# Another issue order for a fused attention and two-MLP kernel on one Trainium2 core

## The chip, the cores and the metric

The kernel runs on one core of one Trainium2 chip. The metric is the device time of one execution in microseconds (us), as a median over runs; the profile is one further execution, taken by the hardware profiler. The engines are TensorE (PE in the rows, with its weight loads as PEld), VectorE (DVE), ScalarE (ACT), GpSimd (POOL) and SyncE (SP, which issues every DMA here).

## What is computed

8192 tokens of width 192 go through three stages:

```python
# 1. attention: per head a softmax over 7 taps, then a causal sum of 7 shifted rows
w = exp(weight_gen - max); w = w / (sum(w) + 1e-9)
x = einsum('bshk,bskhg->bshg', w, x_unf).reshape(8192, 192)
# 2. first MLP
h = x @ moe_w_in            # 192 -> 2048
x = (h / (1 + exp(-h))) @ moe_w_out
# 3. second MLP, its activation a ratio of polynomials
h = x @ moe2_w_in
P = a0 + a1*h + a2*h**2 + a3*h**3
Q = 1 + |b0|*|h| + |b1|*h**2
out = (P / (Q + 1e-6)) @ moe2_w_out
```

The weights arrive as 64-bit floats and are decoded on the chip.

## The kernel before

The tokens are cut into 16 blocks of 512. For every block `attention` (L691) builds the weighted sums, `unit1` (L911) runs the first MLP in 8 units of 256 hidden channels, `between` (L932) hands its result over, `unit2` (L953) runs the second MLP in 8 units, and `finish` (L1016) stores. Every fp32 factor is split in a high and a low part; a product is the sum of three matmuls per weight.

Each step of this is registered once as a named operation with `Plan.op`. The names that the text uses, with u a unit and b a block, written u.b:

- attention: `M`, `m` (products of taps and rows, L742, on POOL or DVE), `p`, `r`, `a` (their sums, L752, L756, L762, on DVE or POOL), `T` and `TR` (the two halves of a transpose on PE, L822), `XH`/`XL` (high and low part of the transposed block, `XH0`/`XL0` for the first MLP on tile tp, `XH1`/`XL1` for the second on tile acc; ACT L839, DVE L843);
- first MLP: `A`, `K` (the two halves of the first product into bank h, PE), `S` (silu, ACT L916), `H`, `L` (high and low part, ACT L920, DVE L924), `C`, `E`, `I`, `F` (second product into acc, PE);
- second MLP: `B`, `Q` (first product), `U`, `V` (ACT L961, L965), `u`, `w`, `Y` (DVE L971, L974, L980), `N`, `G` (ACT L985, L988), `g` (DVE L991), `h`, `l` (high part on POOL, ACT or DVE, low part on DVE or POOL, L1001), `D`, `P`, `J`, `R` (second product);
- decoding of weights, `q` + MLP + matrix + part: `l0`/`l1` loads by DMA, `a0`/`a1` the top bits (ACT L603), `40`/`41` the joining into a PSUM bank (tile dec, DVE L616), `h` the high part (ACT; for matrix B in two steps `h0` and `h1`, L656 and L657), `x` the low part (DVE L637; `x0` and `x1` for matrix B). `q1B` is the 64-row remainder of the second MLP's first matrix;
- softmax chunks `s0` to `s5`, constants `cl`, `ca`, `cr`, `cn`, `cz`.

The order in which all 3956 operations are issued is the string `ORDER` (L40), one entry per operation: `^` or `^^` puts a load of ScalarE's function table before it, `@n` picks the n-th of the engines that the operation allows, `:x` names the buffer slot of a tile that appears there first, and `<n` or `>n` shifts a matmul group of the one half of PE's rows against the other. Each engine runs its own operations in this order, and waits where an input or a buffer is not ready. There are eight PSUM banks in four slots of two (A to D); the tiles h, acc, dec, tp and to share them, so a new tile in a slot waits for the last reader of the tile before.

PE works as two halves of 64 rows, each with its own 64x128 weights, side by side. `Lanes` (L376) merges two queues, one per half, by counted turns. The two row halves must not add into one bank half at the same time, so where a group turns a bank from one side to the other, an empty instruction on SP (L405, `sp.nop`) waits for both halves of the first side, and the second side waits for it:

```python
            if was:
                while any(self.left[n] for n in was[2]):
                    self.take(1 - r)
                step = self.sp.nop()
```

## Time and profile before

| | |
|---|---|
| median of 3 runs | 1211.11 us (1210.18 to 1213.15) |
| the profiled execution | 1208.21 us, of which the span from first to last instruction is 1206.4 us |
| PE matmul busy | 1171.9 us (97%) in 10332 instructions |
| PE weight loads busy | 1038.9 us (86%) |
| DVE busy | 1082.1 us (90%) in 1023 instructions |
| ACT busy | 1035.7 us (86%) in 1011 instructions |
| POOL busy | 508.0 us (42%) in 335 instructions |
| mean granted TensorE clock | 0.996 of full speed |

A matmul's end is modelled, and two of them, one per row half, run at the same time; a busy PE therefore tells that at least one half works.

### The profile page before, as it was taken

What the parts mean: (1) busy time and instruction counts of PE and PEld (TensorE: products, weight loads), DVE (VectorE), ACT (ScalarE), POOL (GpSimd) and SP (SyncE); (2) the same over time, 40 slices, a digit from 0 to 9 for tenths busy, and PEclk for the clock granted to TensorE, in tenths of its full rate; (3) what the DMA queues carried; (4) which work ended last, traced back from release to release, by engine and by line L of the source; (5) the groups of instructions that cost most, each with busy time, mean ns of one, the idle gap of its engine ahead of it and who ended that gap; (6) DMA issues with size and microseconds to landing.
All of it is one profiled execution on the core that took longest, in us unless ns stands there. A gap on an engine that the chain in (4) does not pass through costs nothing.

```text
span 1206.4 us, 24906 instructions
## 1 busy us (share of the span) xinstructions
PE 1171.9 (97%) x10332; PEld 1038.9 (86%) x10332; DVE 1082.1 (90%) x1023; ACT 1035.7 (86%) x1011; POOL 508.0 (42%) x335
## 2 busy tenths in 40 slices
...
GB/s 218 215 129 58 50 1 14 43 1 64 1 38 49 42 23 34 23 17 23 1 56 24 34 60 1 11 55 1 23 1 43 31 1 42 2 24 1 10 1 40
DMA packets 17753, 45.42 MB, mean 38 GB/s; under 512 B 2412, under 2 KB 9194, under 8 KB 17640
## 3 DMA queue, kind: packets, MB, share of 16 engines
...
## 4 chain that ended last, share of the span: by engine, by line
PE 78%; DVE 5%; ACT 4%; issue 1%; POOL 1%; SPq 0%; DMA 0%; DVEq 0%; ACTq 0%; POOLq 0%
PE acc L809 40%; PE h L809 37%; DVE y L980 1%; POOL g2l L1001 1%; DVE t L971 1%; DVE t L974 1%; PE to L1029 1%; ACT y L988 1%; PE tp L822 1%; DVE t L991 1%; ACT y L985 1%; ACT g2h L465 0%; ACT y L965 0%; ACT t L961 0%; ACT g1h L920 0%
## 5 line engine op out<-in xcount | busy, mean ns | idle before, releaser
L809 PE MATMUL h<-xh,wa 64*128 64x512 f32 x2048 | 437.9, 393 | 7.7 <-DVE t L974 4.1
L809 PEld LDWEIGHTS h<-xh,wa 64*128 64x128 f32 x2048 | 277.7, 184 | 44.6 <-SPq L405 7.4
L809 PE MATMUL h<-xh,wb 64*128 64x512 f32 x1024 | 296.9, 388 | 0.0
L809 PE MATMUL h<-xl,wa 64*128 64x512 f32 x1024 | 296.6, 388 | 0.1
L809 PE MATMUL acc<-g2h,wo 64*128 64x512 f32 x1536 | 287.5, 390 | 1.3 <-ACT g2h L465 1.0
L809 PE MATMUL acc<-g1h,wo 64*128 64x512 f32 x1536 | 287.6, 392 | 0.2
L1001 POOL TENSOR_TENSOR g2l<-t,g2h 128x1024 fp32r<-128x1024 f32 x76 | 195.0, 2570 | 136.1 <-ACT g2h L465 36.6
L809 PEld LDWEIGHTS acc<-g2h,wo 64*128 64x128 f32 x1536 | 208.3, 184 | 19.6 <-SPq L405 1.7
L809 PEld LDWEIGHTS acc<-g1h,wo 64*128 64x128 f32 x1536 | 205.2, 185 | 19.1 <-ACT g1h L920 1.2
L809 PE MATMUL acc<-g2l,wo 64*128 64x512 f32 x1024 | 201.4, 391 | 0.1
L809 PE MATMUL acc<-g1l,wo 64*128 64x512 f32 x1024 | 197.0, 394 | 0.2
L924 DVE TENSOR_TENSOR g1l<-h,g1h 128x1024 fp32r<-128x1024 f32 x128 | 155.8, 1220 | 41.3 <-ACT g1h L920 35.9
L980 DVE SCALAR_TENSOR_TENSOR y<-y,b_sb 128x1024 f32<-128x1024 f32 x128 | 175.9, 1381 | 5.6 <-ACT y L965 5.0
L467 POOL TENSOR_SCALAR g2h<-t 128x1024 fp32r<-128x1024 f32 x56 | 68.3, 1223 | 266.2 <-DVE t L991 108.4
L971 DVE TENSOR_TENSOR t<-t,h 128x1024 f32<-128x1024 f32 x128 | 155.3, 1215 | 26.1 <-ACT t L961 13.2
L991 DVE SCALAR_TENSOR_TENSOR t<-t,a_sb,y 128x1024 f32<-128x1024 f32 x128 | 168.4, 1328 | 8.3 <-ACT y L988 7.7
L742 POOL TENSOR_TENSOR pr<-xw,aw 128x576 f32<-128x576 f32 (+1 forms) x73 | 114.4, 1580 | 140.1 <-PE acc L809 83.3
L961 ACT ACTIVATE t<-h,a_sb 128x1024 f32<-128x1024 f32 x128 | 153.8, 1203 | 18.2 <-PE h L809 14.9
L916 ACT ACTIVATE h<-h 128x1024 f32<-128x1024 f32 x128 | 129.3, 1012 | 44.3 <-PE h L809 40.7
L974 DVE SCALAR_TENSOR_TENSOR t<-t,a_sb,h 128x1024 f32<-128x1024 f32 x128 | 163.5, 1279 | 3.7
L965 ACT ACTIVATE y<-h,b_sb 128x1024 f32<-128x1024 f32 x128 | 141.8, 1111 | 25.9 <-PE h L809 20.0
L809 PEld LDWEIGHTS h<-xh,wb 64*128 64x128 f32 x1024 | 149.6, 184 | 10.1
...
## 6 DMA issues: line engine op xcount, KB each, us to landing
...
```

What stands on the lines that cost most here:

```text
L467: pool.tensor_scalar(out=out, in0=in_, scalar1=1.0, scalar2=0.0, op0=ALU.mult, op1=ALU.add)
L742: e.tensor_tensor(out=p.rearrange("p k (h g) -> p k h g", g=G), in0=st[xw][:, j + k0:j + k0 + n, :].rearrange("p k (h g) -> p k h g", g=G) ...
L809: return pe.matmul(out=out, lhsT=w, rhs=x, start=start, stop=stop)
L916: act.activation(out=st[hb], in_=st[hb], func=AF.Silu)
L924: dve.tensor_tensor(out=t, in0=st[hb], in1=st[gh].bitcast(F32), op=ALU.subtract)
L961: act.activation(out=q, in_=st[hb], func=AF.Identity, scale=a_sb[:, 3:4], bias=a_sb[:, 2:3])
L965: act.activation(out=q, in_=st[hb], func=AF.Abs, scale=b_sb[:, 1:2])
L971: dve.tensor_tensor(out=st[t], in0=st[t], in1=flat(), op=ALU.mult)
L974: dve.scalar_tensor_tensor(out=st[t], in0=st[t], scalar=a_sb[:, 1:2], in1=flat(), op0=ALU.add, op1=ALU.mult)
L980: dve.scalar_tensor_tensor(out=st[y], in0=st[y], scalar=b_sb[:, 0:1], in1=st[y], op0=ALU.add, op1=ALU.mult)
L991: dve.scalar_tensor_tensor(out=st[t], in0=st[t], scalar=a_sb[:, 0:1], in1=st[y], op0=ALU.add, op1=ALU.mult)
L1001: e.tensor_tensor(out=q, in0=st[t], in1=st[gh].bitcast(F32), op=ALU.subtract)
```

## The change

Only the string `ORDER` changes; the operations and all functions are the same. Counted in the two strings:

- The operations of every engine come in another order, from the second entry on. 3956 entries stay 3956.
- Loads of ScalarE's function table: 79 before, 89 after.
- Choice of engine: `h` on POOL/ACT/DVE 56/43/29 before, 54/49/25 after; `l` on DVE/POOL 52/76, then 55/73; `p` on DVE/POOL 34/30, then 28/36; `r` on DVE/POOL 30/34, then 25/39; `a` on POOL/DVE 45/19, then 42/22; `M` on POOL/DVE 36/28, then 37/27; `m` 37/27, then 39/25; the evacuations `EC` and `FC` on ACT/DVE 26/6, then 22/10.
- In PE's program, a bank turned to its other side directly after the last matmul of the first side: 16 times before, 7 after. Turns in all: 684 and 669. Neighbouring matmuls or transposes that use the same row half: 224 and 192; from PE's 9600th instruction on, where the program drains, 32 and 12.
- In the decoding of `q1B`, ACT's `h0` stood before DVE's `x1` and now stands behind it. Between `XL0.0` and `q1B0x0` DVE loses M0.1, M1.1, m2.1, r0.1, r1.1 and s1m and receives p0.1, p1.1, p2.1, a3.1, q0O140 and q1O040.
- Up to `XL1.1`, the entry of block 1 into the second MLP, DVE loses M0.1, M1.1, m2.1, m0.3, m2.3, p0.3, p1.3, p2.3, r0.1, r1.1, r1.2, r1.3, s1m, Y7.0, g4.0, g6.0, h2.0 and l0.0 and receives a3.1, a0.2, a2.2, l5.0, p0.1, p1.1, p2.1, p2.2, r3.2 and q0O140. The matmuls ahead of some groups: `T.1` 282 before and 280 after, `B0.0` 376 and 376, `B1.1` 877 and 854, of 9728 in all.
- At the start, `q0B0l1` is loaded ahead of the own rows of block 0 (`Z.0`), and `s2l` behind them. Ahead of `XL0.0` DVE loses s0n and r3.0 (to POOL) and q0O140 (to a later place) and receives s1m.

The start, up to about block 0's entry into the second MLP, and the end, before and after:

```diff
--- before.py
+++ after.py
@@ -38,247 +38,246 @@
-    s0l X.0 s2l:r q0B0l0:x s0m s0d ^^s0e Z.0 cn cz:f s0t s0n M1.0@1:i M0.0@1:y s2m M2.0@1:a q0B0l1:e q0A0l0:h q0B0a0
-    q0B040:B q0A0a0 q0A0l1:l m1.0@1:o q0O0l0:n M3.0@1:q m0.0@1:d p0.0 p1.0 r0.0 m3.0@1:u q0A040:C q0B0a1 q0B041 r1.0
-    a0.0@1:s m2.0@1:m p3.0 r3.0 p2.0 q0A0a1 q0A041 q0O0a0 r2.0 q0O040:D q0B0h0 a2.0 W0.0:A q0B0h1 a3.0 a1.0 q0B0x0
-    q0B0x1 q0A0h q0A0x q0O1l0:j WT.0 q0O0l1:e q0O1a0 q0O0a1 s2d@1 q0O140:C q0O041 XH0.0:d XL0.0:b s1l q0O1l1:m
-    q0A1l1:v W1.0:B s1m q0O1a1 A0.0 q0O141 q0O0h q0A1l0:t q0O0x s1d@1 A1.0:A cl X.1 K0.0 s2e q0O1h@1 s1e s1t q0O1x
-    ^S0.0 s2t s1n@1 K1.0 H0.0:h L0.0:m S1.0 H1.0:n L1.0:w A2.0:D I0.0:C q0O2l1:i K2.0>2 s2n@1 q0O2l0:k q0A1a1 q0A1a0
-    m1.1:p C0.0>2 A3.0:B C1.0 E1.0<2 ca S2.0 H2.0:a E0.0<2 q0A140:A K3.0<2 q0O3l0:q m0.1:h F1.0<2 q0A141 I1.0<2 I2.0
-    L2.0:o F2.0>2 q1O0l0:l q0A1h q0A1x s2s A5.0:A>2 q0O3l1:w q0O2a0 q1B0l1:u q0O2a1 S3.0 E2.0>1 K5.0>1 m3.1:c
-    q0O240:D F0.0 H3.0:j M0.1@1:e I3.0 q0O241 L3.0:y p0.1@1 M2.1:v q0O2h q0O2x S5.0 H5.0:k cr m2.1@1:g A4.0:B>2
-    L5.0:n p2.1@1 q1A0l1:t q1B0l0:s q0O3a0 C2.0>2 q1A0l0:m q0O340:D q0O3a1 q0O341 K4.0 S4.0 M3.1@1:a q0O3h q0O3x
-    A6.0:A C3.0 K6.0<2 E3.0<2 p3.1@1 M1.1@1:w A7.0:D<1 H4.0:h S6.0 H6.0:j C4.0<1 L4.0:i q1O1l0:g K7.0<3 L6.0:q
-    q1B0a0 X.2 q1B0a1 AW.2 C6.0<3 E6.0<3 p1.1@1 E5.0<3 r3.1@1 S7.0 H7.0:c q1B040:B q1B041 r1.1 r0.1 r2.1 q1B0h1 I6.0
-    F4.0>2 F5.0>2 q1A0a1 L7.0:u q1A0a0 a0.1:x F7.0 I4.0 F6.0>2 a3.1 a1.1 F3.0>2 I5.0>2 a2.1 q1O0l1:r q1O1l1:p q1B0h0
-    q1B0x1 E4.0 q1A1l0:b q1A1l1:e q1A040:A q1A041 q1B0x0 q1A0h T.1:B TR.1 I7.0 m0.2:d E7.0 m2.2:t C7.0 C5.0<2 q1O0a0
-    q1O0a1 q1A0x q1O040:D q1O041 q1O1a0 q1O1a1 q1O0h q1O140:A q1O141 q1O0x m3.2:g XH0.1:q XL0.1:y A2.1:D K2.1 q1A1a0
-    q1O1h EC.0:c q1O1x m1.2:a q1A1a1 M3.2:p EM.0 A1.1:A q1A140:B q1A141 S2.1 H2.1:u s3l:o q1A1h AW.3 q1O2l0:n K1.1
-    p3.2 L2.1:j A0.1:D K0.1 r3.2@1 S1.1 EA.0 XH1.0:h q1O2l1:x q1A1x H1.1:c XL1.0:i M0.2:w A3.1:B K3.1 M2.2:k p0.2@1
-    M1.2:v L1.1:s B0.0:C Q0.0 s3m S0.1 q1O2a0 H0.1:g S3.1 H3.1:l q1O2a1 q1O3l0:d q1O240:A L0.1:e r0.2@1 L3.1:b
-    p1.2@1 B5.0:D F1.1:B F2.1 V0.0:a a0.2:n Q5.0 q1O241 r1.2 q1O3l1:x Y0.0 E2.1 E0.1 E3.1 q1O2h X.3 q1O2x U0.0:r
-    B3.0:A F0.1 U5.0:w Q3.0 u0.0 u5.0 I2.1 F3.1>2 w0.0 a1.2 ^^N0.0 w5.0 B2.0:C>2 q1O3a1 U3.0:j p2.2@1 r2.2@1 a3.2
-    u3.0 C2.1>2 G0.0 a2.2 s3d@1 E1.1 q1O3a0 g0.0 V3.0:e V5.0:b Q2.0 m3.3:t w3.0 I1.1 q1O340:D m2.3@1:u I3.1>2
-    h0.0@1:p B1.0:A>2 U2.0:k q1O341 q1O3h Y5.0 q1O3x C1.1>2 Q1.0 V2.0:a u2.0 U1.0:m u1.0 N5.0 w2.0 s3e s3t m1.3:f
...
-    V4.15:j Y4.15 h5.15@1:l u4.15 w4.15 Q7.15>4 h6.15@1:h N4.15 FC.14:n G4.15 l5.15@1:e V7.15:w U7.15:y D5.15>3
-    D3.15 P3.15<2 l6.15:b P5.15 g4.15 Y7.15 u7.15 h4.15@1:f l4.15@1:s N7.15 G7.15 w7.15 g7.15 h7.15@2:w l7.15:p
-    D6.15 P6.15<1 R6.15 J5.15 FT.14:C>2 R5.15>2 J4.15>2 J6.15>4 R4.15 O.13 D4.15 P4.15<2 D7.15<1 P7.15 FR.14 R7.15
-    J7.15 FE.14@1 FA.14 O.14 FC.15:v FT.15:D FR.15 FE0.15 FA0.15 FE1.15@1 O0.15 FA1.15 O1.15
+    s0l cz:f s0m X.0 q0B0l0:h q0B0l1:x Z.0 s0d ^^s0e s0t s0n@1 M2.0@1:a M1.0@1:l q0B0a0 q0B040:B M0.0@1:q q0B0a1
+    q0B041 q0B0h0 m2.0@1:h m0.0@1:r M3.0@1:u m3.0@1:w q0B0h1 m1.0@1:e p2.0 p0.0 r2.0 p1.0 q0A0l0:b q0A0a0 cn
+    q0A040:C W0.0:A r0.0 r1.0 cl q0A0l1:s q0A0a1 q0A041 p3.0 a0.0@1:g s1l q0O0l0:n q0O0a0 ca r3.0@1 a1.0 q0B0x0 a3.0
+    a2.0 q0A0h q0A0x q0O040:D q0B0x1 s2l:k q0O0l1:d q0O1l0:t q0O0a1 q0O1l1:v WT.0 W1.0:B s1m q0O041 q0A1l0:h q0O1a0
+    q0A1l1:e s2m s1d@1 XH0.0:r XL0.0:y cr s2d@1 q0O140:C q0O1a1 q0O0h q0O0x q0O141 s1e s1t q0O1h@1 s2e X.1 q0O1x
+    A0.0 A1.0:A q0A1a0 K0.0 ^S0.0 H0.0:l L0.0:t q0O2l0:c A2.0:D K1.0 S1.0 H1.0:q s1n@1 L1.0:w K2.0 I0.0:C q0O2l1:x
+    q0A140:A S2.0 q0A1a1 q0A141 H2.0:v m3.1:h m1.1:j A3.0:B q0A1h L2.0:d q0A1x q0O3l0:n q0O2a0 I1.0 F0.0>2 F1.0>2
+    K3.0>2 E1.0>2 q1B0l1:a q1B0l0:i S3.0 q0O240:D M3.1@1:o C0.0>2 C1.0 A5.0:A<1 q0O2a1 q0O241 p3.1@1 H3.0:u q0O2h
+    L3.0:l q0O2x F2.0 q0O3a0 q0O3l1:p m0.1:b K5.0 I3.0 F3.0>2 A4.0:B>2 q0O340:D q1A0l0:x C3.0>2 s2t S5.0 H5.0:w K4.0
+    q1B0a0 q1O0l0:s q1A0l1:c q0O3a1 L5.0:m M2.1:g E2.0 E0.0 A6.0:A m2.1:n C5.0 K6.0<2 p2.1 q0O341 F5.0<2 I2.0<2 I5.0
+    S4.0 H4.0:e r2.1 L4.0:t F4.0>2 M1.1:p q1B040:B q0O3h q1B0a1 q0O3x S6.0 A7.0:D>2 q1O0l1:i C2.0>2 q1O1l1:u
+    q1O1l0:d r3.1@1 q1A0a0 H6.0:h q1B041 p1.1 q1B0h1 q1A0a1 K7.0 E4.0 S7.0 H7.0:v E5.0 E3.0 C4.0 M0.1:a L6.0:q
+    C6.0<2 q1A040:A C7.0<4 p0.1 q1A041 q1B0x1 q1A1l0:c r0.1@1 a0.1:j q1A1l1:m L7.0:r q1O0a0 r1.1@1 a3.1@1 q1O040:D
+    q1B0h0 a1.1 q1B0x0 q1O0a1 a2.1 q1A0h F6.0 q1O041 q1A0x q1O0h q1O0x q1O1a0 I6.0 T.1:B q1O140:A s3l:o E7.0 E6.0
+    TR.1 XH0.1:q q1O1a1 F7.0 XL0.1:s q1O141 I7.0 I4.0>2 q1A1a0 EC.0:g q1O1h q1A140:B q1O1x A2.1:D q1A1a1 q1A141
+    q1O2l1:w K2.1 S2.1 s3m H2.1:c EM.0 L2.1:n q1O2l0:t A1.1:A K1.1 q1A1h q1O3l1:d q1O2a1 S1.1 EA.0 XH1.0:h H1.1:p
+    X.2 A0.1:D K0.1 S0.1 H0.1:a q1A1x XL1.0:i s3d@1 q1O2a0 L1.1:x s2n@1 L0.1:g s2s A3.1:B K3.1 S3.1 H3.1:l B0.0:C
+    q1O240:A q1O241 B5.0:D q1O2h q1O3a1 L3.1:y Q0.0 V0.0:e q1O2x Q5.0 E1.1:B C3.1 V5.0:b C1.1<2 U5.0:w AW.2 B3.0:A<4
+    U0.0:v Y0.0 Y5.0 m1.2:t M1.2:u I2.1<4 F1.1<1 q1O3l0:r Q3.0<1 M0.2:m ^^N0.0 U3.0:j F0.1<1 q1O3a0 V3.0:k m2.2:x
+    u5.0 u0.0 w0.0 w5.0 I0.1<1 I1.1>1 B2.0:C>3 q1O340:D u3.0 m0.2:p q1O341 p0.2@1 F2.1>3 F3.1>3 w3.0 Q2.0>3 C0.1>3
...
+    V7.15:p l2.15:h U7.15:n g3.15 B4.15:C h3.15@1:g J2.15 R2.15>2 J5.15>2 Y7.15 N7.15 G7.15 Q4.15>4 V4.15:d R6.14>4
+    P2.15>4 D3.15>4 D2.15>2 l3.15@1:l P5.15 P3.15 U4.15:y u7.15 w7.15 g7.15 R3.15 h7.15@1:s Y4.15 l7.15@1:a N4.15
+    G4.15 u4.15 w4.15 g4.15 h4.15@2:r l4.15:k R6.15 J3.15 R5.15>2 J7.15>2 R7.15 FC.14:t FT.14:C P7.15 D7.15 D4.15<2
+    P4.15 FR.14 R4.15 J4.15 FC.15:u FT.15:D FE.14@1 FA.14 O.14 FR.15 FE1.15 FA1.15 O1.15 FE0.15 FA0.15 O0.15
```

## Rows read from the trace of the kernel before

**Rows 1.** By stretch: us, busy (count) PE, PEld, DVE, ACT, POOL, PEclk, DMA, GB/s
```profile
29.00:85.00 56.00, 50.94 (x392) 39.73 (x394) 49.34 (x70) 45.60 (x58) 32.12 (x29) 0.97 0.60 180
85.00:148.00 63.00, 61.73 (x521) 50.42 (x519) 60.83 (x61) 58.83 (x60) 37.64 (x25) 1.00 0.18 59
148.00:1140.00 992.00, 984.15 (x8815) 885.79 (x8811) 892.66 (x810) 868.66 (x830) 408.70 (x260) 1.00 0.08 24
1140.00:1206.40 66.40, 59.39 (x504) 47.82 (x502) 56.17 (x50) 50.04 (x49) 22.76 (x10) 0.97 0.07 23
```

**Rows 2.** Waits: engine, line, what it awaited; us in total, times, longest
```profile
DVE wb L637 <- ACT wb L657: 2.9, 1, 2.9
PE tp L822 <- DVE t L974: 2.9, 1, 2.9
```

**Rows 3.** PE in time around 68 us: start us, us, engine line op names; idle before
```profile
67.97 1.02 PE L822 MATMUL tp<-ident,ao 64*128 64x64 f32 x16 [2.94 <-DVE wb L637]
...
73.48 0.49 PE L809 MATMUL h<-xh,wa 64*128 64x512 f32 x1
```

**Rows 4.** Busy time by stretch around the wait, PEclk behind the engines
```profile
68.00:70.00 2.00, 1.91 (x22) 1.23 (x22) 1.91 (x3) 1.01 (x2) 0.00 (x0) 0.87 0.30 121
70.00:73.00 3.00, 2.91 (x13) 2.12 (x13) 2.86 (x5) 2.98 (x6) 2.22 (x2) 0.52 0.00 0
```

**Rows 5.** DVE in time, the decoding of the second MLP's first weights
```profile
27.79 1.22 DVE L843 TENSOR_TENSOR xl<-tp,xh 128x1024 fp32r<-128x1024 f32 x1
...
37.82 2.76 DVE L616 SCALAR_TENSOR_TENSOR dec<-raw,tops 128x512 int32<-128x512 int32 x2
...
63.54 1.40 DVE L637 SCALAR_TENSOR_TENSOR wb<-dec,wb 64x512 fp32r<-64x512 f32 x2 [2.90 <-ACT wb L657]
...
66.44 1.38 DVE L637 SCALAR_TENSOR_TENSOR wb<-dec,wb 64x512 fp32r<-64x512 f32 x2
...
73.25 1.21 DVE L843 TENSOR_TENSOR xl<-tp,xh 128x1024 fp32r<-128x1024 f32 x1
```

**Rows 6.** POOL in time beside the joining at 37.82
```profile
37.21 2.82 POOL L742 TENSOR_TENSOR pr<-xw,aw 128x576 f32<-128x576 f32 x2 [0.32 <-PE acc L809]
```

**Rows 7.** PE in time, block 0 enters the second MLP; last row: block 1 does
```profile
85.00 0.62 PE L809 MATMUL h<-xh,wa 64*128 64x512 f32 x4
...
85.92 0.40 PE L809 MATMUL h<-xl,wb 64*128 64x512 f32 x2
86.42 0.73 PE L809 MATMUL h<-xh,wa 64*128 64x512 f32 x4
...
147.91 0.39 PE L809 MATMUL h<-xh,wa 64*128 64x512 f32 x1
```

**Rows 8.** Groups by line and shape: xcount | busy us, mean ns of one | idle before
```profile
L980 DVE SCALAR_TENSOR_TENSOR y<-y,b_sb 128x1024 f32<-128x1024 f32 x128 | 175.9, 1381 | 5.6 <-ACT y L965 5.0
L991 DVE SCALAR_TENSOR_TENSOR t<-t,a_sb,y 128x1024 f32<-128x1024 f32 x128 | 168.4, 1328 | 8.3 <-ACT y L988 7.7
...
L1101 ACT ACT_TABLE_LOAD x40 | 51.3, 1283 | 1.4 <-PEq L1122 0.7
...
L752 POOL TENSOR_TENSOR pr<-pr 128x576 f32<-128x576 f32 x30 | 47.5, 1586 | 38.5 <-DVE pr L742 29.9 <-issue 4.3 <-ACT g1h L920 2.8
L465 ACT ACTIVATE g2h<-t 128x1024 fp32r<-128x1024 f32 x43 | 45.1, 1056 | 4.0 <-POOL g2l L1001 1.9 <-DVE t L991 1.8
...
L742 DVE TENSOR_TENSOR pr<-xw,aw 128x768 f32<-128x768 f32 x28 | 26.9, 966 | 2.0 <-DMA xw<-in_x_dram 1.3 <-PE acc L809 0.7
L752 DVE TENSOR_TENSOR pr<-pr 128x576 f32<-128x576 f32 x34 | 26.7, 791 | 0.3 <-POOL pr L742 0.2
L742 DVE TENSOR_TENSOR pr<-xw,aw 128x576 f32<-128x576 f32 x27 | 22.4, 833 | 0.4 <-PE acc L809 0.4
...
L756 DVE TENSOR_TENSOR pr<-pr 128x384 f32<-128x384 f32 x30 | 16.4, 553 | 0.1
...
L616 DVE SCALAR_TENSOR_TENSOR dec<-raw,tops 128x384 int32<-128x384 int32 x16 | 10.3, 646 | 0.4
```

431 lines of the change are left out of this document (216 added, 215 removed).

## The prediction

> **What bounds the kernel now.** I first read busy time by stretch [rows 1]. In the long middle, 148 to 1140 us, PE is busy 984.15 of 992 us. DVE with 892.66 and ACT with 868.66 have a tenth or more to spare; another order can win back a few us there at most. The beginning is different: from 29 to 85 us PE is idle for 5.1 us and DVE for 6.7, while the weights are decoded. From 85 to 148 us DVE works 60.83 of 63 us and ACT 58.83: the elementwise engines pace PE. The last 66.4 us, in which the pipeline drains, leave PE idle for 7.0. So the change is costed in four stretches, and the first two decide.
>
> Then the waits [rows 2]. Two of them last 2.9 us each and are links of one chain: PE, about to transpose block 1, waits for DVE's low part of the weights wb, and DVE had waited for ACT's high part of wb. In order of time, PE starts that transpose at 67.97 after 2.94 us of idleness and reaches block 1's first product only at 73.48 [rows 3]. Behind the gap the granted clock is 0.87 over 68 to 70 us and 0.52 over 70 to 73 [rows 4]: the lower of the two levels, 1.2 instead of 2.4 GHz. That costs 0.13 x 2 + 0.48 x 3 = 1.7 us of full-speed work.
>
> On DVE the gap stands ahead of the pair at 63.54 [rows 5]. This pair is x1, which needs only h1 by its data; h1 and h0 fill different columns of wb. Yet it waits for h0, because it stands behind h0 in the program and both read the same PSUM tile. Its partner x0 follows at 66.44 and ends at 67.82; the bank is then free for the transpose.
> The Trainium skill, PSUM — Partial Sum Buffer, PSUM bank collisions raise a hardware error, says that ScalarE and VectorE may not read one bank in the same quadrant together and that software has to order them. By that rule the wait is not removed but turned round: h0 has to wait for x1, and up to 1.4 us (the pair at 66.44) of the gain come back, which would make the first term below -3.1 instead of -4.5. The row agrees that the readers are kept apart; whether h0 pays for it no row shows, since here it came first.
>
> **First stretch, up to block 0's entry into the second MLP.** The start is costed at nothing: DVE carries it, and there it loses three short operations and receives one, under 1 us together. Loading q0B0l1 before Z.0 delays the own rows; two early multiplies and the first joinings cover that. Without cover it is about 1 us. I keep -1 to +1.3.
>
> From XL0.0 (27.79) to x0, DVE loses two M, one m, two r and s1m, 2 x 0.966 + 0.833 + 2 x 0.553 = 3.9 us and s1m, and receives three p, two joinings and one a, 3 x 0.791 + 2 x 0.646 = 3.7 us and a [rows 8]. That is a draw. What goes is the idle 2.90 us: x1 now stands ahead of h0, and between them ACT has S7, H7 and a0 to do, while DVE has L7, a3 and a joining. Hence x0 ends near 64.9 and the transpose starts 3.0 us earlier.
> PE comes to the transpose earlier too, since its units are fed earlier, so it will still wait for x0, one to two us by my count. A wait of 2.9 us on the same kind of transpose, later in the kernel [rows 2], left the mean clock of the middle at 1.00 [rows 1]; so a short wait need not bring the low clock, and I take it as gone.
> Behind x0, DVE has four operations ahead of XL0.1 instead of six, two joinings fewer: 5.4 - 1.3 = 4.1 us, so XL0.1 starts at 69.0 instead of 73.25, 4.3 earlier. PE has 24 matmuls at 0.115 (eight from 85.00 to 85.92 [rows 7]) and two transposes of half a us, 3.8 us at full clock instead of the 5.5 from 67.97 to 73.48, and so is there at 68.7. The chain up to B0.0 (85.00) keeps its length: EC, its swap by DMA, EA, XL1.0; s3m is in and p3.2 is out, both near 1 us. SP's queue holds X.2 and the loads of the late weights between the empty instructions that turn PE's banks; each of these loads waits for a slot that is freed before PE needs the next turn, which I costed at nothing (a late one would hold PE by its delay, 1 us or so).
> Term: **-4.5 us**, between 0 (the wait finds another place) and -6.5 (idle 2.94, low clock 1.7, and 1.9 of the 2.1 in other short gaps).
>
> **Second stretch, to block 1's entry.** From 85.00 to 147.91 [rows 7] PE does 501 matmuls and one transpose pair: 57.6 + 1.0 = 58.6 us of work in 62.9, so 4.3 are lost. Now 478 matmuls (854 - 376) stand there, 56.0 us. Up to XL1.1 DVE sheds, net, 2 M, 3 m, 3 r, 1 Y, 2 g less 1 p: 1.93 + 2.50 + 1.66 + 1.38 + 2.66 - 0.79 = 9.3 us, less two short ones (0.65 each), 8.0 [rows 8]; some 0.5 of it lies before B0.0. DVE has then 60.8 - 7.5 = 53.3 us against PE's 56.0 and no longer paces it. Three direct turns of a bank fewer save 0.27 each (86.42 - 85.92 - 0.23 [rows 7]), but every small wait still shows with both engines nearly full. Term: **-2 us**, between -4.3 (all that is lost) and +3.
>
> **Middle.** PE lost 7.9 us here. The ten more table loads are 10 x 1.283 = 12.8 us and six more h on ACT 6 x 1.056 = 6.3 [rows 8], 19.1 at most, beside ACT's 123 us of idle time [rows 1]. They are hidden while ACT waits for PE; where ACT is late, each costs up to 1.28. DVE has to make up the work that it shed early, 8.0 less the 2.6 that belong to 23 matmuls, 5.4 us in its 99 us of slack. Term: **+1 us**, between -6 (most of the idle PE time recovered) and +8.
>
> **End.** Twenty neighbours fewer on one row half let 20 x 0.115 = 2.3 us of matmuls overlap, and three direct turns fewer 0.8; but DVE and ACT are full there, and block 14 leaves DVE one operation more behind EA.15 (about 1.3). Term: **-1 us**, between -3.4 and +2.
>
> **Sum.** 0 - 4.5 - 2 + 1 - 1 = -6.5: 1208.21 becomes 1201.7 for the profiled execution. That one was 2.9 us under the median 1211.11, so the median goes to **1204.6**.
>
> **Rivals.**
> - *The wait persists* (chance 0.12): DVE or ACT reaches the decoding of q1B no earlier, a load or a tile slot being late, and PE idles about 3 us at another place with the low clock behind it. The first term is then 0: 1209. For it: in this stretch DVE and ACT are never idle for long, and a wait can slip to the next link. Against it: the order on DVE and ACT around h0 and x1 really differs.
> - *Given back* (0.15): DVE's 5.4 us of shed work come back while PE needs them, 1204.6 + 5.4 = 1210. For it: DVE is at 90% in the middle. Against it: 10% of slack return 5.4 us within 60.
> - *ACT becomes the bound* (0.13; slower): in the middle, table loads and h come between PE's finished bank h and S, whose H feeds the next C; PE then waits on ACT. Up to 19.1 us lie there. From about 10.2 of them on PE's path the kernel is slower than before by over 0.3%; three quarters give 1204.6 + 14 = 1219. For it: 86% busy become 88%, and in 85 to 148 us ACT had 4.2 us left of 63. Against it: 123 us idle in the middle.
> - *DVE held by POOL* (0.06): six p and five r go from DVE to POOL. The joining pair at 37.82 took 2.76 us, against 0.646 for one of three quarters the width [rows 8], while POOL's products ran from 37.21 on for 2.82 [rows 5, 6]. If the moved sums hold DVE for half their length, six at 1.586 and five priced no higher, that is 8.7 us at most: 1213. Most fall in stretches where DVE has slack.
> The Trainium skill, SBUF — State Buffer, section SBUF: two separate sides, has VectorE and GpSimd share a port pair that whoever starts first holds for the whole instruction; by that rule the moved sums only look cheap. The joining pair agrees with it.
>
> **How the numbers follow.** My forecast, 1199 to 1208, has 0.54. About 0.3% (3.6 us) is what a measurement of this kernel can tell from no change. Faster, below 1207.5: 0.52 of the forecast, 0.03 each of the first two rivals, 0.58. Slower, above 1214.7: 0.11 of ACT's, 0.03 of the others', 0.14. The rest, 0.28, is within. The range reaches from 1196, with the two early terms at their low bounds (-4.3) and the other two half way to theirs (-4.7), to 1213, the POOL case; ACT's case and some of the low end stay outside.
>
> **What would show it.** Right: the first product of block 1 starts near 69 and B0.0 near 80.5, the clock stays at 1.00 after 30 us, DVE has no gap of 2 us in 55 to 75, block 1's entry (now the 855th matmul) is near 139. The middle's PE idle stays under 10 us and the drain's near 6. Wrong: a gap of PE over 2 us followed by a low clock; PE waiting on ACT's H or S in the middle by more than a few us; joinings or sums on DVE lengthened in 30 to 75 us.

## The result and the profile after

| | before | after |
|---|---|---|
| median | 1211.44 us (1210.18 to 1213.15) | 1195.19 us (1194.63 to 1195.47) |
| the profiled execution | 1208.21, span 1206.4 | 1195.10, span 1193.3 |
| PE busy in the span | 1171.9 (97%) | 1164.3 (98%) |
| DVE, ACT, POOL busy | 1082.1, 1035.7, 508.0 | 1091.2, 1049.3, 518.1 |
| mean granted clock of the profiled execution | 0.996 | 0.998 |

After stands to before as 0.9864, 95% interval 0.9847 to 0.9881: 16 us faster. The forecast was 1204.6 with a range from 1196; the result lies 0.8 us below that range.

Line numbers of after are one lower than those of before; in the experiments' kernels, whose order is wrapped otherwise, they are four lower. First the windows of after, cut at the same events as those of before [rows 1]: to the first product of block 0 in the second MLP, to block 1's entry, to the 9240th matmul or so, to the end. The columns are those of [rows 1].

```profile
29.00:79.60 50.60, 48.23 (x394) 38.84 (x392) 46.70 (x68) 45.54 (x57) 22.16 (x20) 1.00 0.63 196
79.60:138.00 58.40, 57.06 (x498) 51.92 (x494) 56.28 (x54) 55.81 (x56) 36.20 (x23) 1.00 0.06 15
138.00:1127.00 989.00, 983.33 (x8803) 910.46 (x8805) 908.45 (x811) 879.69 (x839) 420.09 (x270) 1.00 0.09 27
1127.00:1193.30 66.30, 60.45 (x539) 56.35 (x535) 57.96 (x53) 55.21 (x56) 30.73 (x12) 0.97 0.07 23
```

PE is idle for 2.4 us of the first stretch (5.1 before), 1.3 of the second (1.3 of a longer one before, paced by DVE), 5.7 of the middle (7.9) and 5.9 of the drain (7.0). DVE and ACT have more to do in the middle than before, and PE less to wait for.

The waits of PE in after, from the view that sums them (engine, line, what was awaited, total us, times, longest), beside [rows 2]:

```profile
PE h L808 <- DVE t L973: 2.7, 4, 0.9
PE h L808 <- DVE g1l L923: 1.7, 3, 0.8
PE acc L808 <- DVE xl L842: 1.5, 1, 1.5
...
PE h L774 <- ACT xh L838: 1.1, 1, 1.1
...
PE tp L821 <- DVE wb L636: 0.5, 1, 0.5
```

PE's wait for `wb` ahead of the transpose, 2.94 in [rows 3], is 0.5; VectorE's wait for ScalarE's `wb`, the first in [rows 2], and that of `tp` for `t`, the second, are gone. PE waits for ACT for 1.1 us at the start and as long at the end, not in between, and behind the start no wait in the list is longer than 1.5.

PE's timeline of after around T.1 and at block 0's entry, and VectorE's and ScalarE's ahead of it (start, length, instruction, count, in brackets the idle time before):

```profile
64.62 0.46 PE L821 MATMUL tp<-ident,ao 64*128 64x64 f32 x8 [0.53 <-DVE wb L636]
...
67.66 0.50 PE L808 MATMUL h<-xh,wa 64*128 64x512 f32 x1
...
79.57 0.62 PE L808 MATMUL h<-xh,wa 64*128 64x512 f32 x4
```

```profile
59.27 1.40 DVE L636 SCALAR_TENSOR_TENSOR wb<-dec,wb 64x512 fp32r<-64x512 f32 x2
60.70 1.23 DVE L923 TENSOR_TENSOR g1l<-h,g1h 128x1024 fp32r<-128x1024 f32 x1
...
63.09 1.38 DVE L636 SCALAR_TENSOR_TENSOR wb<-dec,wb 64x512 fp32r<-64x512 f32 x2
...
67.41 1.23 DVE L842 TENSOR_TENSOR xl<-tp,xh 128x1024 fp32r<-128x1024 f32 x1
```

```profile
60.14 0.64 ACT L602 ACTIVATE tops<-raw 128x384 f16<-128x384 bf16 x1
60.70 1.02 ACT L655 ACTIVATE wb<-dec 64x1024 fp32r<-64x1024 f32 x1
61.74 0.59 ACT L656 ACTIVATE wb<-dec 64x512 fp32r<-64x512 f32 x1
```

x1 (59.27) runs ahead of h0 (60.70), which starts the moment x1 ends and has no idle time in front. The transpose begins at 64.62 where it began at 67.97, block 1's first product at 67.66 (73.48 in [rows 3]), B0.0 at 79.57 (85.00 in [rows 7]).

The same matmul by its number in PE's program, start in us, shows where the 13 us of the two profiled executions arise; a number that stays constant from one row to the next is a stretch in which nothing is won or lost on balance:

| matmul | before | after | difference |
|---|---|---|---|
| 1st | 28.90 | 28.70 | -0.2 |
| 377th (B0.0) | 85.00 | 79.57 | -5.4 |
| 855th | 145.21 | 137.99 | -7.2 |
| 5001st | 635.04 | 625.88 | -9.2 |
| 9001st | 1108.61 | 1099.65 | -9.0 |
| 9241st | 1136.53 | 1126.99 | -9.5 |
| end of the span | 1206.40 | 1193.32 | -13.1 |

The first product's start varies from 27.6 to 29.4 us among the traces of all kernels here, so the first row tells nothing of the order. The medians lie 16.25 us apart, 3.1 more than the two profiled executions: before's profiled one was 3.2 us under the median of the table, after's lies on its median.

### The profile page after: what moved, and what is told of

It is laid out like the page before. It is cut to its first block, busy times and chain, and to the rows that moved or that the text cites. A ratio compares the mean times of both kernels' runs of the same rounds, so it can differ in the third digit from the quotient of the medians.

```text
span 1193.3 us, 24919 instructions
## 1 busy us (share of the span) xinstructions
PE 1164.3 (98%) x10332; PEld 1072.2 (90%) x10332; DVE 1091.2 (91%) x1016; ACT 1049.3 (88%) x1023; POOL 518.1 (43%) x340
## 4 chain that ended last, share of the span: by engine, by line
PE 84%; DVE 5%; ACT 4%; issue 2%; SPq 0%; DVEq 0%; ACTq 0%
PE acc L808 44%; PE h L808 39%; DVE y L979 1%; ACT h L915 1%; DVE g1l L923 1%; ACT g1h L919 1%; PE to L1028 1%; PE tp L821 1%; DVE t L970 1%; DVE t L990 0%; DVE t L973 0%; DVE g2l L1000 0%; ACT L1102 0%; ACT y L964 0%; ACT t L960 0%
## 5 line engine op out<-in xcount | busy, mean ns | idle before, releaser
L808 PE MATMUL h<-xh,wa 64*128 64x512 f32 x2048 | 433.2, 393 | 6.6 <-DVE t L973 2.7
L808 PEld LDWEIGHTS h<-xh,wa 64*128 64x128 f32 x2048 | 274.7, 184 | 37.2 <-issue 4.9
L808 PE MATMUL h<-xh,wb 64*128 64x512 f32 x1024 | 293.5, 388 | 0.0
L808 PE MATMUL h<-xl,wa 64*128 64x512 f32 x1024 | 293.2, 388 | 0.0
L808 PE MATMUL acc<-g2h,wo 64*128 64x512 f32 x1536 | 282.4, 390 | 0.0
L1000 POOL TENSOR_TENSOR g2l<-t,g2h 128x1024 fp32r<-128x1024 f32 x73 | 188.7, 2594 | 167.5 <-ACT g2h L464 55.0
L808 PEld LDWEIGHTS acc<-g1h,wo 64*128 64x128 f32 x1536 | 209.1, 184 | 11.5 <-ACT g1h L919 0.5
L808 PE MATMUL acc<-g1l,wo 64*128 64x512 f32 x1024 | 202.9, 391 | 0.6 <-DVE g1l L923 0.4
L990 DVE SCALAR_TENSOR_TENSOR t<-t,a_sb,y 128x1024 f32<-128x1024 f32 x128 | 173.2, 1363 | 8.4 <-ACT y L987 7.7
L808 PEld LDWEIGHTS h<-xl,wa 64*128 64x128 f32 x1024 | 151.1, 184 | 7.4 <-DVE xl L842 0.3
```

Source lines behind the costliest of these rows:

```text
L808: return pe.matmul(out=out, lhsT=w, rhs=x, start=start, stop=stop)
L990: dve.scalar_tensor_tensor(out=st[t], in0=st[t], scalar=a_sb[:, 0:1], in1=st[y], op0=ALU.add, op1=ALU.mult)
L1000: e.tensor_tensor(out=q, in0=st[t], in1=st[gh].bitcast(F32), op=ALU.subtract)
```

## The experiments

Medians stand against the runs of before on the same chip: 1211.41 us for swap_x1, early_new, tail_new and early_tail_new, 1209.81 for t14_later, l3_dve, swap_t14 and drain_old, 1210.96 for first_new, half_new, half_old and after_plus, and 1211.49 for after_h0x1, after_loads and after_plus2. After itself was run beside the 1211.44 of the result. "Lead" is the difference of the same matmul's start to before's profiled execution. A kernel that joins two orders takes the first one's entries up to a matmul and then the remaining entries as the second orders them; where a buffer slot is still held there, a free one is named.

**The exchange of h0 and x1, alone and undone.**

```diff
-q1B0h0 q1B0x1
+q1B0x1 q1B0h0
```

> The kernel before with two neighbouring entries exchanged: q1B0x1 now stands ahead of q1B0h0; nothing else. Theory (the order of the two readers made the early gap): DVE's x1 starts near 60.7 instead of 63.5, ACT's h0 waits under 0.2 us for it, x0 ends near 65, the transpose of block 1 starts near 65.1 instead of 68.0, no low clock behind it, block 1's first product near 69 instead of 73.5; the whole 3 to 5 us faster than before, 1207 or so against a median of 1211. Rival (the wait is only turned round): h0 is delayed by 1.4 us or more, x0 ends near 66.5, the gap stays at 1.5 us or more with the low clock behind it; under 2 us faster. Rival (given back): early gain as in the theory, but under 1 us of it left at the end.

Measured: 1208.03 us, ratio 0.9971 (0.9961 to 0.9981), as the theory had it. ScalarE's h0 waits 0.31 us for x1, so the wait is hardly turned round. T.1's wait is 0.7 us instead of 2.9, the half-speed stretch behind it is absent, and from B0.0 to the 8000th matmul the lead stays between 2.0 and 3.0 us. At the end it is 0.5, because of T.14. The windows of swap_x1 behind T.1's place, around T.14, and behind it:

```profile
69.00:72.00 3.00, 2.13 (x14) 1.16 (x10) 3.00 (x5) 3.00 (x5) 3.00 (x3) 1.00 0.03 12
...
996.00:1000.00 4.00, 2.93 (x20) 2.70 (x22) 3.96 (x4) 2.59 (x3) 0.00 (x0) 0.65 0.01 4
1000.00:1004.00 4.00, 4.00 (x40) 3.85 (x39) 2.15 (x3) 1.94 (x3) 0.72 (x1) 0.92 0.06 12
```

The same wait for the same instruction in before's profiled execution:

```profile
996.00:1000.00 4.00, 1.11 (x14) 0.69 (x12) 3.96 (x4) 3.19 (x4) 0.00 (x0) 1.00 0.00 0
1000.00:1004.00 4.00, 4.00 (x46) 3.67 (x44) 3.96 (x4) 2.08 (x3) 0.00 (x0) 1.00 0.01 4
```

After three idle us the clock fell to 1.2 GHz in the one execution (0.65 and 0.92 as means of 4 us, 0.35 x 4 + 0.08 x 4 = 1.7 us lost) and stayed at 2.4 in the other. The prediction read only the second.

In the changed kernel the exchange was undone:

```diff
-C7.0<4 p0.1 q1A041 q1B0x1 q1A1l0:c ... q1O040:D q1B0h0 a1.1 q1B0x0
+C7.0<4 p0.1 q1A041 q1A1l0:c ... q1O040:D q1B0h0 q1B0x1 a1.1 q1B0x0
```

> The changed kernel with the decoding of q1B put back into the order of before: VectorE's x1 behind ScalarE's h0, three VectorE operations later than now. Theory (in the changed kernel VectorE reaches this place some 4 us earlier than in before, so that the exchange is worth only part of the first step): T.1 0.5 to 1.5 us later, the shift carried to the end, median 1195.5 to 1197. Rival (the exchange is the first step): T.1 2.2 to 3.6 us later as in before, 1197.4 to 1199 on the median, with half-speed stretches behind T.1 in some executions and runs 2 to 4 us apart.

Measured: 1197.10 us, 1.9 more than after. PE's and VectorE's timeline, and two windows:

```profile
64.42 0.50 PE L818 MATMUL tp<-ident,ao 64*128 64x64 f32 x8 [1.64 <-DVE wb L633]
```

```profile
61.47 2.79 DVE L633 SCALAR_TENSOR_TENSOR wb<-dec,wb 64x512 fp32r<-64x512 f32 x4
```

```profile
60.00:65.00 5.00, 3.18 (x25) 2.17 (x25) 4.93 (x9) 2.72 (x5) 1.82 (x3) 0.97 0.73 225
65.00:69.00 4.00, 4.00 (x30) 3.58 (x29) 3.02 (x5) 2.93 (x5) 0.00 (x0) 0.61 0.24 63
```

T.1 waits 1.64 us instead of 0.53. Measured from each kernel's own first product, the transpose is only 0.4 us later; but the clock falls to 1.2 GHz behind the wait (0.03 x 5 + 0.39 x 4 = 1.7 us lost), so the 304th matmul, in block 1's first product, is 1.9 later, and the end of the span 2.4. Theory and rival are each right in one half: T.1 hardly moves, and the half-speed stretch is there. Of the four runs the three with a mean clock of 0.997 or 0.998 take 1196.9 to 1197.8 us; the one with 0.999 takes 1195.36, no more than after. What undoing the exchange costs here is thus nearly all clock.

Both runs put the exchange at some 2 us, in different ways. Alone in before it brings B0.0 forward by 2.0 us, counted from the first product; taken out of after it costs 1.9 there. After's B0.0 comes 5.2 us earlier than before's, counted in the same way, so the moved work has the other 3.2. Beside [rows 5], swap_x1's x0 and XL0.1 show where, and one joining of before with GpSimd beside it:

```profile
63.99 1.38 DVE L633 SCALAR_TENSOR_TENSOR wb<-dec,wb 64x512 fp32r<-64x512 f32 x2
...
70.80 1.21 DVE L839 TENSOR_TENSOR xl<-tp,xh 128x1024 fp32r<-128x1024 f32 x1
```

```profile
70.79 1.61 DVE L616 SCALAR_TENSOR_TENSOR dec<-raw,tops 128x384 int32<-128x384 int32 x1
```

```profile
70.78 1.21 POOL L742 TENSOR_TENSOR pr<-xw,aw 128x576 f32<-128x576 f32 x1 [3.03 <-DVE dec L616]
```

XL0.1 starts 5.43 us behind x0's end in before and in swap_x1, and 2.94 in after. Two joinings fewer are 1.2 of these 2.5 us. Another 1.1 are the joining of 1.61 us, where its like take 0.55: it starts 0.01 us behind a product on GpSimd and ends 0.4 behind that one's end, as if held by it. In after GpSimd does nothing there. x0 itself ends 0.9 us earlier than in swap_x1 (64.47 against 65.37).

**The wait of T.14.** The trace of before shows VectorE's Y7.12 at 3.43 us, where the median Y takes 1.28, and beside it l3.12 on GpSimd:

```profile
993.35 3.43 DVE L980 SCALAR_TENSOR_TENSOR y<-y,b_sb 128x1024 f32<-128x1024 f32 x1
```

```profile
993.19 2.51 POOL L1001 TENSOR_TENSOR g2l<-t,g2h 128x1024 fp32r<-128x1024 f32 x1
```

w7.12, which frees T.14's bank, stands behind Y7.12. Three kernels:

```diff
 # t14_later
-J0.12>2 T.14:A>4 u6.12 w6.12 F7.13>4 Y6.12 g7.12 G5.12 F6.13>4 I7.13>4 TR.14>6 D1.12>6 D0.12>4 EC.13:s P0.12>2
+J0.12>2 F7.13>4 u6.12 w6.12 F6.13>4 I7.13>4 Y6.12 g7.12 G5.12 D1.12>4 D0.12>4 T.14:A>4 EC.13:s P0.12>4 TR.14>2
 # l3_dve
-l3.12@1:i u7.12 w7.12 ... u6.12 w6.12
+u7.12 w7.12 ... u6.12 w6.12 l3.12:i
 # swap_t14: the edits of swap_x1 and of t14_later
```

> The kernel before, with the transpose T.14/TR.14 placed behind F7.13, F6.13, I7.13, D1.12 and D0.12 on TensorE, so that it no longer stands for 2.9 us in front of work that was ready. Theory (a wait of TensorE costs its own length at the place where it stands, the shift is carried to the end, and in some executions a half-speed stretch of 3.4 us behind it costs 1.7 us more): the stall at 996 us falls to under 0.7, the trace runs 2 to 3 us ahead from 1003 us to the end, the median falls from 1211.4 to 1207 to 1209. Rival (what is won is given back at the next wait, since DVE's chain behind it is as late as before): a new stall of 2 to 3 us within 20 us, median 1210 to 1212.

> The kernel before, with one subtraction, l3.12, moved from GpSimd to VectorE behind w6.12. In the trace of before it ran on GpSimd from 993.2 to 995.7 us, and VectorE's Y7.12 beside it took 3.43 us where the median Y takes 1.28; T.14 waits for the w7.12 behind it. Theory (GpSimd held VectorE there, and that made the wait): Y7.12 takes 1.3 us, T.14's wait falls from 2.9 to about 0.8 us, median 1207 to 1209.5. Rival (Y7.12 was long because it waited for ScalarE's V7.12): Y7.12 keeps its 3.4 us, the wait stays at 2.9, and VectorE has 1.2 us more to do: median 1211 to 1213.

> Both waits of 2.9 us of the kernel before taken away: q1B0x1 ahead of q1B0h0 as in swap_x1, and T.14 later as in t14_later. Theory (two independent local waits, each with its half-speed stretch in some executions): -2.2 and -2.9 us in the trace, up to 1.7 us more for each on the median: 1202.5 to 1206, mean granted clock 0.998, and runs that lie within 2 us of each other as after's do. Rival (the half-speed stretches come at the same rate without those waits): median 1206 to 1207, clock 0.993 to 0.997, runs 4 to 6 us apart as before's.

Measured: t14_later 1209.38 us, ratio 0.9993 (0.9983 to 1.0002), short of its expectation; l3_dve 1207.66, ratio 0.9979 (0.9969 to 0.9988); swap_t14 1204.27, ratio 0.9949 (0.9932 to 0.9965).

t14_later, one line of the waits of PE (in all, times, longest):

```profile
PE h L805 <- DVE xl L839: 2.5, 3, 1.6
```

l3_dve, VectorE:

```profile
995.65 1.27 DVE L976 SCALAR_TENSOR_TENSOR y<-y,b_sb 128x1024 f32<-128x1024 f32 x1
996.85 1.21 DVE L967 TENSOR_TENSOR t<-t,h 128x1024 f32<-128x1024 f32 x1
```

In before Y7.12 ends at 996.78, 1.1 us behind the end of l3.12 (993.19 + 2.51 = 995.70), as if it had begun only there; without l3.12 it takes 1.27 in all. So GpSimd held VectorE, by 2.15 us: T.14's wait is 0.7 in l3_dve instead of 2.9. In the trace the lead rises by 2.15 at T.14, and 0.7 of it is gone again by 1008 us; the median falls by 2.15, with an interval that reaches from 1.5 to 3.8. The rival, a wait for ScalarE's V7.12, has fallen. The Trainium skill, SBUF — State Buffer, section SBUF: two separate sides, says just this of an instruction on VectorE with two inputs in SBUF: it shares a port pair with a GpSimd instruction that reads SBUF, and whoever starts first holds it for the whole instruction. This run agrees, with 2.15 us.

t14_later takes the stall away and pays most of it back at once: XL0.14, whose input the transpose is, is as late as before, A1.14 waits 1.6 us for it, and of the 2.9 us only 0.4 are left in the trace at 1008 us. Here the rival was right, and the median agrees with it.

swap_t14 has both edits. Its median, 5.5 us under before, is as expected; its trace, 3.2 us ahead at the end, is not, as T.14's move is worth 0.4 there. The rest fits executions without the two half-speed stretches: its runs lie 2.5 us apart, with clocks of 0.996 to 0.999.

**Halves of the order.**

```diff
 # half_old: before up to the 5102nd matmul, then after (23 slots renamed)
 # half_new: after up to the 5102nd, then before (145 slots renamed)
 # first_new: after up to the 304th, then before (95 slots renamed)
 # early_new: after up to the 1500th, then before
```

> The order of before up to the 5102nd matmul, then after's. Theory (local, additive): no lead at the cut, the seam's cost there, then 3.9 us ahead at the end in the trace (T.14's wait gone, after's drain kept) and up to 1.7 us more on the median for the half-speed stretch behind T.14: 1205 to 1207. Rival (after's second half is only good behind its own first half): no lead outside the seam, 1209 to 1213.

> After's order up to the 5102nd matmul, then the order of before. Theory (leads are local to their places and add up): 9.2 us ahead at the cut as the two traces show, the seam's cost subtracted there, then carried unchanged to the end with before's wait of T.14 and before's drain: 1201 to 1204, with the runs 3 to 5 us apart because of T.14's wait. Rival (before's second half gives some of it back): the lead shrinks from the cut to the end by over 2 us outside the 200 matmuls around the seam.

> After's order up to TensorE's 304th matmul (the first product of block 1), then the order of before. Theory (what the new order wins ahead of that place, 5.6 us in the two traces, is a shift that the rest carries to the end): the trace runs 5 to 6 us ahead of before's from 74 us to 1206 us less what the seam costs, and the median falls from 1210 to 1211 by 5 to 7 us, to 1204 to 1206. Rival (the lead is given back at the next entry, since the second MLP's decoded weights come as late as before): the lead shrinks to 1 or 2 us by the 376th matmul, median 1208 to 1211.

> The changed order up to 1500 of the 9728 product matmuls (about 214 us), then every remaining operation in the order of before; 17 tiles at the seam take another buffer slot. Theory (the early stretches give 7.5 us, independent of what follows): 7 to 8 us faster than before, 1204; the lead of about 7.5 us over before at 220 us stays to the end. Rival (given back): the order of before behind it needs the work that was put off, the lead shrinks by the 5.4 us of DVE work to 2 us, 1209.

Measured: half_old 1204.52 us, ratio 0.9951 (0.9934 to 0.9969), just under the 1205 to 1207 expected. Its lead is -0.7 at the 5000th matmul (0.7 us late, with a longer half-speed stretch behind T.1), -0.3 at the 9240th and 3.4 at the end; T.14's place alone takes it from -2.5 to 0.6. So after's second half is worth 6.4 us on the median by itself: 4.1 in the trace; that the rest is T.14's low clock in before's other executions fits, but is not shown.

The other three came out slower than before: half_new 1217.95, first_new 1219.38, early_new 1225.54. All three hold the expected lead up to the cut (10.9 us at the 5000th matmul, 6.3 at the 304th, 7.8 at the 1500th) and lose it in one or a few stalls behind it, one line of PE's waits for each, in this order:

```profile
PE h L805 <- DVE g1l L920: 6.6, 6, 3.0
```

```profile
PE h L805 <- DVE g1l L920: 7.7, 3, 6.4
```

```profile
PE acc L805 <- POOL g2l L997: 15.4, 1, 15.4
```

Behind the long waits the clock is at 1.2 GHz for 10.2 us in first_new and 13.7 in early_new, which costs 5.1 and 6.8 us more. In first_new, L2.1 stands behind p3.2 on VectorE, and p3.2 behind five products of taps on GpSimd, from 71.4 to 77.7 us, most of which before's order places ahead of the cut. These are costs of the seam, not of the order; half_new goes on losing behind it, too (11 us from the 6000th to the 9000th matmul). Some 5.5 of these are a wait of 2.1 us at 873.6 and the half-speed stretches behind it and behind T.14's wait; the rest is not settled, and its 145 renamed slots are a suspect. So the first half's 9.8 us are known by difference only (16.25 - 6.4), with 10.9 and 7.8 us of lead at the two cuts beside them.

**The drain.**

```diff
 # tail_new: before up to the 9240th matmul, then after
 # drain_old: after up to the 9208th, then before
 # early_tail_new: after up to the 1500th, before up to the 9240th, then after
```

> The order of before up to 9240 of the 9728 product matmuls (about 1137 us), then every remaining operation in the changed order; 11 tiles at the seam take another slot. Theory (the drain's gain comes from its own order: fewer neighbouring matmuls on one row half and one low part fewer on DVE): 3 to 4 us faster than before, 1208. Rival (the drain was faster since the changed middle hands it a better state): under 1 us faster.

> After's order up to TensorE's 9208th matmul, then the order of before. Theory (the 3.6 us that after wins in the drain belong to its order there): 1195.2 + 3.6 = 1198.8 us, with before's stalls of the drain back (8 us of row time behind 1150 us against 3.7). Rival (the drain's order is worth nothing by itself, and its gain comes from the state in which the middle leaves the engines): 1194.5 to 1196. The seam at the cut may add up to some us; if so, it stands between the 9208th and the 9300th matmul and is told apart there.

> The changed order up to 1500 matmuls, that of before up to 9240, the changed one again for the drain. Theory (three independent terms, early -7.5, middle -2, drain -3.5): the sum of early_new and tail_new, 11 us faster than before, 1200, and 4 to 5 us slower than the changed kernel by the middle and by two seams. Rival (the terms are not independent): the sum of the two single gains is missed by over 2 us.

Measured: tail_new 1214.80 us, ratio 1.0025 (1.0012 to 1.0038); drain_old 1207.43, 12 more than after; early_tail_new 1228.73, with early_new's loss in it. tail_new and drain_old miss both theory and rival. early_tail_new misses its 1200, but is the sum of the two single changes to 0.2 us: 14.1 and 3.4 us slower than before by themselves, 17.3 together. drain_old loses 11 us at its seam (two waits, 4.1 and 2.1 us, and 5.1 us of low clock behind them) and cannot give a median for the drain. Behind the seam it does speak: from the 9400th matmul to the end before's order takes the time that it takes in before, to 0.3 us. tail_new, after's order behind before's middle, loses 4 us from the 9240th matmul to the end, with a new wait of 2.2 us ahead of 1173.3 and 1.7 us of low clock behind it. half_old, after's order behind after's last blocks, wins 3.7 us there (0.3 late to 3.4 ahead), as after does. So the 3.6 us of the drain belong to the drain together with the blocks ahead of it, not to the last entries alone; which property of the two makes them is not shown.

**Ten more table loads in after.**

```diff
-H0.3 ... H3.4 ... H4.5 ... V7.5 ... U1.13
+^H0.3 ... ^H3.4 ... ^H4.5 ... ^^V7.5 ... ^^U1.13
```

> The changed kernel with ten more loads of ScalarE's function table, each of the table already there, spread evenly from block 2 to block 13 ahead of five H, three V and two other operations: 12.8 us more work for ScalarE, which is busy for 880 of 989 us in the middle. Theory (ScalarE's loads lie in its idle time, and only those ahead of an operation that TensorE awaits soon cost part of their 1.28 us): 0 to 4 us, median 1195.2 to 1199. Rival (ScalarE is near enough to the bound that each load is paid in full): 12 us or more, median above 1206.

Measured: 1201.72 us (1201.18 to 1202.47), 6.5 more than after: 0.65 us for a load of 1.283. Both expectations missed, one below and one above. The middle of after_loads, beside the third of the windows above:

```profile
138.00:1127.00 989.00, 979.45 (x8741) 901.97 (x8739) 901.31 (x805) 884.98 (x842) 419.85 (x270) 1.00 0.09 27
```

PE is idle for 9.6 us here instead of 5.7, in many small gaps, and gets 62 matmuls less done in the same 989 us. ACT has 104 us free and still passes half of each load on. That an H or V that is late is at once a late product would explain it; it was not followed from load to load.

**A better order.** In after's trace three stalls of the middle are over 1 us from one matmul's start to the next: C5.5 to R1.4 at 404.9 (Y3.4 took 3.46 us on VectorE beside l0.4 on GpSimd), K4.12 to A5.12 at 892.0, C7.14 to B6.13 at 1051.0 (h1.13 took 2.77 beside l4.13).

```diff
 # after_plus
-l0.4@1:c V4.4:k ... u4.4 w4.4
+V4.4:k ... u4.4 w4.4 l0.4:c
-M2.13@1:j r0.13 u5.11 w5.11
+r0.13 u5.11 w5.11 M2.13@1:j
-l4.13@1:n E7.14 ... u7.13 w7.13
+E7.14 ... u7.13 w7.13 l4.13:s
 # after_plus2, in addition
-l3.11@1:l goes from GpSimd to VectorE, behind L7.12
-N4.14 h5.14@1:o G4.14 ... I6.15<2 u4.14 EC.15:l
+N4.14 ... I6.15<2 EC.15:l h5.14@1:o G4.14 u4.14
```

> The changed kernel with three operations moved at its three longest stalls of the middle. l0.4 goes from GpSimd to VectorE behind w4.4 (Y3.4 took 3.46 us beside it; the stall C5.5 to R1.4 at 404.8 us is 1.75), l4.13 from GpSimd to VectorE behind w7.13 (h1.13 took 2.77 us beside it where 0.69 is usual; the stall C7.14 to B6.13 at 1050.8 us is 1.06), and M2.13 goes behind u5.11 and w5.11 on VectorE (K4.12 to A5.12 waits 1.04 us for w5.11). Theory (a wait that VectorE is held in by GpSimd, and that stands on TensorE's path, is worth its length): the three stalls fall below 0.3 us each, 2.5 to 3.8 us in all, median 1191.4 to 1192.7. Rival (each gain turns into a wait at the next place, as half of T.14's did): 1193.5 to 1195.5.

> after_plus with its two new stalls mended: l3.11 goes from GpSimd to VectorE behind L7.12 (beside it Y5.11 took 3.47 us in after_plus, where it takes 1.28 in after; stall of 2.14 us before F7.12), and ScalarE's EC.15 goes ahead of h5.14 and G4.14 (B6.14 waits 1.44 us for the bank that it frees). Theory: 2 us less for the first and 0.6 to 1.4 for the second, median 1189.5 to 1191. Rival (further waits take their place): 1192.5 to 1194.

Measured: after_plus 1193.17 us (1191.47 to 1194.71), after_plus2 1192.43 (1191.52 to 1192.77), ratio to before 0.9844 (0.9830 to 0.9859); after_plus2 is 2.8 us under after and has the lowest median of all, though its interval overlaps that of after. Both fall short of their theories: after_plus lies between theory and rival, after_plus2 at the rival. The three stalls are gone in after_plus, but others came: with everything some us earlier, Y5.11 and l3.11 start together. VectorE and GpSimd in after_plus:

```profile
904.24 3.47 DVE L976 SCALAR_TENSOR_TENSOR y<-y,b_sb 128x1024 f32<-128x1024 f32 x1
907.63 1.21 DVE L920 TENSOR_TENSOR g1l<-h,g1h 128x1024 fp32r<-128x1024 f32 x1
```

```profile
904.23 2.40 POOL L997 TENSOR_TENSOR g2l<-t,g2h 128x1024 fp32r<-128x1024 f32 x1 [2.13 <-ACT g2h L461]
```

The same two in after, where VectorE was first:

```profile
907.31 1.28 DVE L979 SCALAR_TENSOR_TENSOR y<-y,b_sb 128x1024 f32<-128x1024 f32 x1
```

```profile
907.64 3.22 POOL L1000 TENSOR_TENSOR g2l<-t,g2h 128x1024 fp32r<-128x1024 f32 x1 [2.47 <-ACT g2h L464]
```

Whichever comes second waits: 2.2 us for VectorE in the one, 0.8 for GpSimd in the other. With 0.01 us between the two starts, a shift decides. In after_plus PE waits 1.76 us behind this Y5.11, and the clock is low behind that, 1.7 us more:

```profile
909.00:912.00 3.00, 3.00 (x16) 2.43 (x18) 2.38 (x3) 2.54 (x3) 0.00 (x0) 0.56 0.00 0
```

after_plus2 moved this l3.11, and the stall behind it went. The second repair failed: the bank of B6.14 was not waiting for EC.15, as read, but for w4.14. PE in after_plus2:

```profile
1125.98 0.73 PE L805 MATMUL h<-xh,wa 64*128 64x512 f32 x4 [1.13 <-DVE t L970]
```

That is a lead given back: at the 9240th matmul after_plus2 is 3.5 us ahead of after, at the 9400th 2.3.

## Why the prediction was right and wrong

**First stretch: right.** -4.5 was forecast, -5.4 measured. Each mark came: x0 ended at 64.47 (64.9 forecast), PE waited for it (0.53 us, not the one to two forecast), the first product of block 1 stood at 67.66 (69), B0.0 at 79.57 (80.5), and the clock was 1.00. Part of the mechanism was off in size. Of the 4.3 us by which XL0.1 was to come earlier, 3.0 were the idle time ahead of x1 and 1.3 two joinings fewer; it came 5.8 earlier (67.41 against 73.25), 3.4 up to x0's end and 2.5 behind it, where the long joining beside GpSimd went as well. The exchange alone gives 2.0 of the gain at B0.0, the moved work 3.2. That no low clock followed goes with a wait shorter than forecast, which was luck: behind 1.64 us, a wait such as the prediction still expected, after_h0x1 lost 1.7 us to it. By the rule on banks that the prediction drew from the Trainium skill, PSUM — Partial Sum Buffer, section PSUM bank collisions raise a hardware error, it let h0 wait for x1 at up to 1.4 us; the trace keeps the readers apart (x1 to 60.67, h0 from 60.70), but ScalarE was busy with top bits of q1O until then, so h0 paid nothing, and 0.31 us in swap_x1.

**Second stretch: right in size.** -2 was forecast, -1.8 measured, block 1's entry at 137.99 (139). The reason given holds only in part: DVE was to come down to 53.3 us and pace PE no longer, but does 56.28 of 58.4, as full as before, and PE is idle for 1.3 as before.

**Middle: the wrong sign.** +1 was forecast, -2.3 measured (7.2 to 9.5 in the table). The lead is 7.4 us ahead of T.14's place and 10.5 behind it, so that place gives 3.1, and all the rest of the middle, loads and postponed work included, takes 0.8. The term weighed loads, h on ACT and VectorE's postponed work against each other and put T.14's wait at nothing. It stood in [rows 2] with 2.9 us: the prediction first read the two rows there as links of one chain, though the second, `tp` for `t`, is T.14's, and then used it as an argument on the clock and not as a gain. Its cause, VectorE held by GpSimd, was even among the rivals, but put where sums had been moved. After's order has l3.12 on VectorE, as l3_dve has, and w7.12 ahead of Y7.12. The loads did have a price to fear: ten more cost 6.5 us in after, half of the length of each. After's own ten are within the 0.8; that their places make the difference is argued, not shown.

**End: undersized.** -1 was forecast, -3.6 measured, 0.2 beyond the term's lower bound. Overlap of row halves 2.3 and direct turns 0.8 were worked out and then discounted by 2 us because "DVE and ACT are full there". They were not: [rows 1] leaves DVE 10 and ACT 16 us free of 66.4, and in after they have 8 and 11 free of 66.3. That the sum without the discount, 3.1, comes near the time does not show its mechanism: tail_new has after's drain behind before's middle and loses 4 us there.

**From the profiled execution to the median: the step that left the range.** 2.9 us were added, as before's median lay that far above its profiled execution. For after, nothing is to be added; without the 2.9 the forecast is 1201.7, its range begins at 1193.1, and the result lies inside. The distance goes back to before's two long waits, where before's profiled execution got off lightly: 1.2 GHz for 3.4 us behind T.1, 1.7 us lost, and none behind T.14. tail_new has before's order up to the 9240th matmul. In its trace the clock is low for 6.8 us behind T.1's wait and for 3.4 behind T.14's, 5.1 us lost, and it reaches that matmul 2.8 us later than before's profiled execution:

```profile
69.00:72.00 3.00, 2.91 (x12) 1.81 (x12) 2.86 (x4) 2.98 (x5) 1.75 (x2) 0.50 0.00 0
72.00:75.00 3.00, 3.00 (x15) 2.32 (x14) 3.00 (x6) 1.18 (x3) 2.43 (x2) 0.50 0.00 0
...
1000.00:1004.00 4.00, 3.52 (x27) 3.28 (x29) 3.96 (x5) 2.01 (x3) 0.00 (x0) 0.57 0.00 0
```

Seven traces have T.14's wait (before, swap_x1, half_new, first_new, early_new, early_tail_new, tail_new); before's is the only one without low clock behind it. Five have T.1's wait of 2.9 to 3.3 us (before, t14_later, l3_dve, half_old, tail_new); before's is the only one with 3.4 us of low clock behind it, the others have 6.8. Over the 58 runs of before beside the experiments the time goes with the mean granted clock: 1212.8 us median at 0.991 (5 runs), 1211.1 at 0.992 (5) and at 0.993 (22), 1209.7 at 0.994 (18), 1209.4 at 0.996 (6); the profiled execution has 0.996.

The sentence that failed is "a short wait need not bring the low clock": it was read from one execution, and that was the exception. Both waits gone, the four runs of after lie within 0.9 us at 0.998 and 0.999. Taken out of before together, the two waits with their low clock are worth 5.5 us on the median (swap_t14).

Of the 9.4 us between forecast and result, this step is 2.8, the middle 3.3, the end 2.6, the first stretch 0.9, and the second -0.2.

**The rivals.** That the wait persists fell at once. That the gain is given back fell for the large leads, which run on over 8000 matmuls; it holds in small places, as at A1.14 in t14_later and B6.14 in after_plus2. That ACT becomes the bound fell, though ten more loads cost 6.5 us. That DVE is held by POOL is true as a mechanism, in before as in after, and the hold at T.14, and by its look the one at the joining ahead of XL0.1, turned out to be part of the gain.
